# Nine layer norms transposed by VectorE through DRAM, the second MLP matmuls one tile later, and one group's reads spread out

## The chip, the cores and the metric

The kernel runs on one core of a Trainium2 chip. The metric is the device time of one execution in microseconds (us). The time before is the median of three runs. "Span" is the time from the first to the last instruction of the profiled execution.

## What is computed

Two pairs of layers run one after the other on 2048 tokens of width 512: attention with 32 heads of width 16, then a dense layer of 1792 features with the Mish activation. Each of the four starts with a layer norm of its input and adds its result to it.

```python
x = x + A(layernorm(x));  x = x + B(layernorm(x))      # twice, with the same weights
# A: qkv = x @ wqkv; p = softmax(q k^T / 4); o = p v; o @ wo
# B: h = x @ w1 + b1; act = h * tanh(softplus(h)); act @ w2
```

## The kernel before

**Tiling.** The tokens are cut into four chunks `c` of 512, each of four blocks of 128. TensorE (PE) contracts over partitions, so each norm's result is needed with features on the partitions: 4 tiles of 128 features by 512 tokens, each split into a high part `th` and the rest `tl`. A product takes three matmuls (high by high, high by low, low by high), which is `mm3` at L176 to L181.

**A norm** is `norm_parts` (L183). VectorE (DVE) takes the statistics (L211, L212), GpSimd (POOL) the root (L190, L191), DVE scales 128 tokens to `xn` (L201), PE transposes them in four matmuls with an identity into one PSUM bank (L247), ScalarE (ACT) copies the bank to `th` (L173) and DVE subtracts to get `tl` (L174). The names are `tpm`, `thm` for the norms ahead of the MLP and `tpq`, `thq` for those ahead of attention. `spread` hangs a norm's steps on the MLP's tiles. It is used for nine norms: chunks 1 to 3 ahead of each MLP, and chunks 0 to 2 ahead of the second attention, which run within the last chunk of the first MLP.

**Attention's input.** `qkv` goes through 32 (feature tile, chunk) pairs `(m, c)`, each 12 matmuls into one of three PSUM banks of the pool "s". ACT and DVE split the bank into `pt` (L173, L174), and ACT's DMA queue writes it to DRAM as `scr` (L525). As soon as m = 0 and 4 are done for all chunks, `prep_qk(0)` reads the first group of heads back. It has 28 steps of one DMA each. The first 14 (two heads) go out on the queues of SP and POOL, the last 14 on ACT's queue and in program order. `2 * PREP` = 14 steps are taken at once, and then two after each further pair. From m = 6 on, `some_max` takes row maxima of the scores in between (PE L336, DVE L340).

**The MLP** runs 14 feature tiles `f` for each chunk in turn. `hid` is 12 matmuls of w1 (L179 to L181, `h`), followed by a chain of ACT, DVE and POOL instructions that makes `ah` (L659) and `al` (L661). `outp` is 12 matmuls of w2 (L673, `mo`), the first 8 with `ah`, the last 4 with `al`. `LAG` = 2 sets the order: after `hid` of tile i and its hooks comes `outp` of tile i - 2. The buffers `he` and `hr` are single, `hb`, `ah` and `al` double.

**The first tiles of an MLP.** The output projection of the last chunk of attention is not ready when the MLP starts. Its operands come by DMA (`num`, and `rec` through POOL's queue), DVE multiplies them (L604), ACT copies the product to `oh` (L610) and DVE subtracts to get `ol` (L611). Its 48 matmuls with wo are hung in four quarters of 12 on tiles 5 to 8 of chunk 0, right after `hid` and ahead of that step's `outp`. The third matmul of a quarter reads `ol`.

**Order.** All PE instructions stand in program order, which `att.pe` fixes. Those given to `behind` (or a `pin`) keep program order too. The rest is placed by a scheduler from its own model of times, and each engine and DMA queue then works through its list in that fixed order.

Of the kernel before, what the change touches and what calls it, by code (L numbers as in the profile page):

```python
# [9 lines left out]
F32 = mybir.dt.float32  # L10
# [8 lines left out]
P = 128  # L19
# [22 lines left out]
PRE = 4  # L42
FILL = 12
KEEP = 2
PREP = 7
WARM = (4, 1, 1)
GSTEPS = NCH * NKT
STEPS = NG * GSTEPS
HEADS = STEPS * HG
LAG = 2  # L50
MAX_M = (6, 3, 7)
T_BUFS = {"he": 1, "hr": 1}
NBLK = 22
# [15 lines left out]
def kernel(ctx: ExitStack, tc: tile.TileContext, x, wqkv, wo, w1, b1, w2, out):  # L69
# [24 lines left out]
    def b8(shape, dt, name):  # L94
        return blk.tile(shape, dt, tag="blk", name=name)
# [18 lines left out]
    def t512(tag, name, dt=F32):  # L114
        return tmp.tile([P, 512], dt, tag=tag, name=name, bufs=T_BUFS.get(tag, 2))
# [60 lines left out]
    def mm3(acc, pairs, first=True, last=True, pe=lambda ins: ins):  # L176
        n = len(pairs)
        for i, (ah, al, bh, bl) in enumerate(pairs):
            pe(nc.tensor.matmul(acc, ah, bh, start=first and i == 0, stop=False))  # L179
            pe(nc.tensor.matmul(acc, ah, bl, start=False, stop=False))  # L180
            pe(nc.tensor.matmul(acc, al, bh, start=False, stop=last and i == n - 1))  # L181

    def norm_parts(src, nm, got, key, tag, fine=False, pin=lambda ins: ins, pe=lambda ins: ins, halves=False):  # L183
        st = tmp.tile([P, NCH, 6], F32, tag="st", name=f"st{nm}")
        mv = tmp.tile([P, NCH, 2], F32, tag="mv", name=f"mv{nm}")
        ve = tmp.tile([P, NCH], F32, tag="ve", name=f"ve{nm}")
        rs = tmp.tile([P, NCH], F32, tag="rs", name=f"rs{nm}")

        def rstd(t, n):
            nc.gpsimd.tensor_scalar(ve[:, t : t + n], mv[:, t : t + n, 1], EPS, None, op0=ALU.add)  # L190
            nc.gpsimd.tensor_tensor(rs[:, t : t + n], ve[:, t : t + n], mhalf[:, t : t + n], op=ALU.pow)  # L191

        xns = []

        def scaled(t, tag):
            if tag == "raw":
                xn = tmp.tile([P, 2, 512], F32, tag=tag, name=f"xn{nm}{t}", bufs=3)[:, 0]
            else:
                xn = t512(tag, f"xn{nm}{t}")
            pin(  # L200
                nc.vector.tensor_scalar(  # L201
                    xn, src[:, t], mv[:, t, 0:1], rs[:, t : t + 1], op0=ALU.subtract, op1=ALU.mult
                )
            )
            return xn

        def next_scaled():
            xns.append(scaled(len(xns), ("f", "ah")[len(xns) // 2]))

        for t in range(NCH):  # L210
            pin(nc.vector.bn_stats(st[:, t], src[:, t]))  # L211
            pin(nc.vector.bn_aggr(mv[:, t], st[:, t]))  # L212
            if fine:
                rstd(t, 1)
                if t and tag == "mx":
                    next_scaled()
        if not fine:
            rstd(0, NCH)
        yield
        th = b8([P, KT, CW], F32R, f"th{nm}")  # L220
        tl = b8([P, KT, CW], F32R, f"tl{nm}")
        got[key] = (th, tl)
        if tag == "mx":
            while len(xns) < NCH:
                next_scaled()
            yield
            for u in range(NCH // 2):
                tp = ps.tile([P, 2, 512], F32, tag=tag, name=f"tp{nm}{u}")
                for e in range(2):
                    for k in range(KT):  # L230
                        pe(nc.tensor.transpose(tp[:, e, ts(k, P)], xns[2 * u + e][:, ts(k, P)], ident))
                two = ts(u, 2 * P)
                split_psum(
                    th[:, :, two].rearrange("p k (t n) -> p k t n", n=P),
                    tl[:, :, two].rearrange("p k (t n) -> p k t n", n=P),
                    tp.rearrange("p t (k n) -> p k t n", n=P),
                    pin,
                )
                yield
            return  # L240
        for t in range(NCH):
            xn = scaled(t, "raw" if tag == "acc" else "f")
            if halves:
                yield
            tp = pbank(tag, f"tp{nm}{t}")
            for k in range(KT):
                pe(nc.tensor.transpose(tp[:, ts(k, P)], xn[:, ts(k, P)], ident))  # L247
            split_psum(th[:, :, ts(t, P)], tl[:, :, ts(t, P)], tp.rearrange("p (k n) -> p k n", k=KT), pin)
            yield

    def spread(hooks, c, f0, src, nm, got, key, pe):
        parts = norm_parts(src, nm, got, key, "acc", pe=pe, halves=True)
        for i in range(2 * NCH + 1):
            hooks.setdefault((c, f0 + i // 2), []).append(lambda: next(parts, None))

    class Attention:
        def __init__(self, l, scr):
# [18 lines left out]

        def prep_qk(self, g):
            l = self.l
            ks, qs = [], []
            for u in range(HG // 2):  # L280
                k = b8([P, S], F32R, f"ks{l}{g}{u}")
                q = b8([P, S], F32R, f"qs{l}{g}{u}")
                m, h0 = divmod(g * HG + 2 * u, P // DH)
                for e in range(2):
                    r0 = e * HALF
                    queue = nc.sync
                    pin = lambda ins: ins
                    if g == 0 and u:
                        queue, pin = nc.scalar, behind
                    elif g == 0 and e:  # L290
                        queue = nc.gpsimd
                    pin(queue.dma_start(
                        k[r0 + KROWS : r0 + MROWS].bitcast(F32).rearrange("p (r n) -> p r n", n=P),
                        minus[:, None, :].to_broadcast([MROWS - KROWS, S // P, P]),
                    ))
                    yield
                    for t, parts, base in ((k, K_PARTS, NCH), (q, Q_PARTS, 0)):
                        for j, a in enumerate(parts):
                            pin(queue.dma_start(
                                t[r0 + j * DH : r0 + (j + 1) * DH].bitcast(F32),  # L300
                                self.scr[base + m][a, (h0 + e) * DH : (h0 + e + 1) * DH, :].bitcast(F32),
                            ))
                            yield
                ks.append(k)
                qs.append(q)
            self.qk[g] = (ks, qs)

        def prep_v(self, g, cs=range(NCH)):
            if g not in self.va:
# [113 lines left out]
        def drain(self):  # L423
            b, self.full = self.full, None
            if b is None:
                return
            g, qb = divmod(b, NCH)
            ot = t512("f", f"ot{self.l}{b}")
            nc.scalar.activation(ot, self.accs.pop(b), AF.Copy)
            nc.sync.dma_start(self.oscr[qb][g // 2, g % 2], ot)  # L430

        def run(self, hooks, pre, fill):
# [203 lines left out]
    def mlp(l, x2s, w1t, w2t, tts, dst, hooks, pe):  # L636
        acts, obs = {}, {}

        def hid(c, f):
            th, tl = tts[c]  # L640
            w = w1t[f // 2]
            acc = pbank("s", f"h{l}{c}{f}")
            mm3(
                acc,
                [(w[:, 0, k, ts(f % 2, P)], w[:, 1, k, ts(f % 2, P)], th[:, k, :], tl[:, k, :]) for k in range(KT)],
                pe=pe,
            )
            nm = f"{l}{c}{f}"
            hb, e, r = t512("f", "hb" + nm), t512("he", "he" + nm), t512("hr", "hr" + nm)
            nc.scalar.activation(hb, acc, AF.Identity, bias=b1t[:, f : f + 1])  # L650
            nc.vector.tensor_scalar(e, hb, HCLAMP, None, op0=ALU.min)  # L651
            nc.scalar.activation(e, e, AF.Exp)  # L652
            nc.vector.scalar_tensor_tensor(e, e, 2.0, e, op0=ALU.add, op1=ALU.mult)  # L653
            nc.scalar.activation(r, e, AF.Ln, bias=1.0, scale=0.5)  # L654
            nc.scalar.activation(r, r, AF.Exp, bias=lnhalf, scale=-1.0)  # L655
            mul = nc.vector if (l, c) == (1, NCH - 1) and f >= FT - 2 else nc.gpsimd
            mul.tensor_tensor(hb, hb, e, op=ALU.mult)  # L657
            ah, al = t512("ah", "ah" + nm, F32R), t512("al", "al" + nm, F32R)
            nc.vector.tensor_tensor(ah, hb, r, op=ALU.mult)  # L659
            mul.tensor_tensor(hb, hb, r, op=ALU.mult)  # L660
            nc.vector.tensor_tensor(al, hb, ah.bitcast(F32), op=ALU.subtract)  # L661
            acts[c, f] = (ah, al)

        def outp(c, f):
# [81 lines left out]
    for l in range(2):  # L746
# [96 lines left out]
            on(f2, lambda i=i: load_w2(i - 1))  # L843
        on(9, lambda: load_w2(6))
        for c in range(NCH - 1):
            spread(hooks, c, 5 if c else 0, x2s[c + 1], f"m{l}{c + 1}", tts, c + 1, att.pe)
        wts, tt = {}, {}
        if l == 0:
            last = NCH - 1
            for f, js in ((2, (0,)), (4, (2,)), (9, (1,)), (11, (3,)), (12, (4,)), (13, (5,))):  # L850
                hooks.setdefault((last, f), []).append(lambda js=js: load_qkv(1, wts, js, splits))
            for c in range(last):
                spread(hooks, last, 1 + 4 * c, x2s[c], f"q1{c}", tt, c, att.pe)
        mlp(l, x2s, w1t, w2t, tts, xs if l == 0 else out, hooks, att.pe)
    close_banks()

# [27 lines left out]
```

## Time and profile before

| | |
|---|---|
| median of three runs (lowest, highest) | 3557.0 us (3555.14, 3560.2) |
| the profiled execution: time, span | 3557.3 us, 3555.5 us |
| matmul instructions | 28716 |
| VectorE, ScalarE, POOL busy | 83%, 71%, 15% of the span |
| first attention's input | about 8 to 120 us |
| first attention, with its output projection | to about 1449 us |
| first MLP | 1449 to 1789 us |
| second attention's input, second attention | to about 3220 us |
| second MLP | 3220 to 3554 us |

In a timeline row the first number is the start, the second the duration, and the brackets hold how long the engine sat idle before the row and what ended that. Matmuls overlap, so their spacing counts and not their duration: the span divided by 28716 is not the cost of any of them, while two neighbours of 512 columns start 0.23 us apart.

### The profile page before, as it was taken

Reading aid. Unit: us, or ns where it says so; the run is one execution under the profiler, and the core shown is the slowest. Engines: PE = TensorE matmul, PEld = TensorE weight load, DVE = VectorE, ACT = ScalarE, POOL = GpSimd, SP = SyncE. Lnnn points to the kernel's source line nnn. Section 1 sums busy time; section 2 is a strip of 40 time slices with the busy share of each in tenths; the row PEclk is TensorE's granted clock in tenths of the full one; section 3 lists DMA queues with packets and bytes.
Section 4 is the critical chain, followed back from the end, with each engine's and each line's share of the span. In section 5 each row is a group of like instructions: output and inputs, shape, how many; then the busy total and the mean of one; then the engine's idle time right before and its main releaser. Section 6 shows DMA issues by size and latency. Waiting matters only on the chain.

```text
span 3555.5 us, 69179 instructions
## 1 busy us (share of the span) xinstructions
PE 3531.8 (99%) x28716; PEld 1940.7 (55%) x28716; DVE 2941.3 (83%) x3016; ACT 2522.2 (71%) x3401; POOL 532.8 (15%) x612
## 2 busy tenths in 40 slices
PE   9999999999999999999999999999999999999999
PEld 7644444444444444788776444444444444447887
DVE  5789999999999994656646999999999999946544
ACT  3188888888888887344422888888888888873444
POOL 3100000000100002444411000000000000024443
PEclk9999999999999999999999999999999999999999
DMA  7641312213132124500164212112021111246000
GB/s 249 219 97 47 83 44 76 61 51 71 46 78 49 42 80 70 186 32 13 60 214 146 53 31 45 38 29 44 29 38 38 41 35 35 74 74 202 13 13 24
DMA packets 139430, 255.11 MB, mean 72 GB/s; under 512 B 29348, under 2 KB 73316, under 8 KB 125292
## 3 DMA queue, kind: packets, MB, share of 16 engines
q1 hardware_dynamic: 112196, 174.04, 19.5%
q10 hardware_dynamic: 19176, 43.06, 3.4%
q0 software_dynamic: 7744, 33.60, 3.4%
q8 instruction: 225, 3.69, 0.5%
q14 instruction: 89, 0.73, 0.1%
HBM read 149.43 MB, written 100.14 MB: 70 GB/s over the span
## 4 chain that ended last, share of the span: by engine, by line
PE 95%; DVE 2%; DMA 2%; issue 1%; ACT 1%; POOL 1%; ACTq 0%; DVEq 0%; SPq 0%; POOLq 0%
PE pv L410 30%; PE pm L336 17%; PE ss L394 12%; PE sp L384 9%; PE mo L673 8%; PE h L179 3%; PE h L181 3%; PE h L180 3%; PE qk L179 1%; PE qk L180 1%; PE qk L181 1%; PE va L179 1%; PE wo L179 1%; DMA scr<-pt 1%; PE va L181 1%
## 5 line engine op out<-in xcount | busy, mean ns | idle before, releaser
L340 DVE TENSOR_REDUCE mxv<-pm 128x2 f32<-128x1024 f32 x2048 | 2385.8, 1219 | 137.3 <-PE pm L336 86.9
L385 ACT ACTIVATE p<-sp 128x1024 f32<-128x1024 f32 x1366 | 1395.9, 1022 | 19.6 <-PE sp L384 15.7
L410 PE MATMUL pv<-p,va 128*32 128x256 f32 (+2 forms) x16032 | 1166.9, 392 | 0.1
L336 PE MATMUL pm<-ks,qs 48*128 48x512 f32 x4096 | 1095.5, 446 | 0.4
L395 ACT ACTIVATE p<-ss 128x512 f32<-128x512 f32 x1364 | 815.1, 598 | 347.4 <-PE ss L394 254.9
L384 PE MATMUL sp<-qs,ks 50*128 50x512 f32 x2732 | 724.8, 446 | 0.7 <-ACT p L385 0.4
L336 PEld LDWEIGHTS pm<-ks,qs 48*128 48x128 f32 x4096 | 451.1, 184 | 345.7 <-issue 171.3
L410 PEld LDWEIGHTS pv<-p,va 128*32 128x32 f32 x16032 | 367.7, 108 | 494.7 <-issue 416.9
L394 PE MATMUL ss<-qs,ks 50*128 50x512 f32 x1364 | 611.4, 448 | 0.0
L394 PEld LDWEIGHTS ss<-qs,ks 50*128 50x128 f32 x1364 | 252.0, 185 | 329.5 <-ACT p L395 225.5
L384 PEld LDWEIGHTS sp<-qs,ks 50*128 50x128 f32 x2732 | 261.2, 183 | 202.4 <-ACT p L385 120.3
L355 POOL CAST np<-nt 128x32 fp32r<-128x32 f32 x64 | 13.4, 210 | 2213.2 <-DVE nt L353 2213.2
L659 DVE TENSOR_TENSOR ah<-hb,hr 128x512 fp32r<-128x512 f32 x112 | 77.3, 690 | 137.2 <-ACT hr L655 89.0
L650 ACT ACTIVATE hb<-h,b1t 128x512 f32<-128x512 f32 x112 | 77.1, 688 | 142.4 <-PE h L181 140.3
L657 POOL TENSOR_TENSOR hb<-hb,he 128x512 f32<-128x512 f32 x110 | 145.7, 1325 | 205.1 <-DVE he L653 202.6
L660 POOL TENSOR_TENSOR hb<-hb,hr 128x512 f32<-128x512 f32 x110 | 147.3, 1339 | 123.7 <-DVE ah L659 123.7
L654 ACT ACTIVATE hr<-he 128x512 f32<-128x512 f32 x112 | 70.8, 632 | 109.8 <-DVE he L653 94.7
L173 ACT ACTIVATE pt<-qk 128x512 fp32r<-128x512 f32 x64 | 38.0, 597 | 154.0 <-PE qk L181 110.9
L652 ACT ACTIVATE he<-he 128x512 f32<-128x512 f32 x112 | 70.8, 632 | 93.5 <-DVE he L651 89.1
L651 DVE TENSOR_SCALAR he<-hb 128x512 f32<-128x512 f32 x112 | 69.3, 619 | 79.9 <-ACT hb L650 77.5
L661 DVE TENSOR_TENSOR al<-hb,ah 128x512 fp32r<-128x512 f32 x112 | 83.0, 741 | 24.7 <-POOL hb L660 24.5
L174 DVE TENSOR_TENSOR pt<-qk,pt 128x512 fp32r<-128x512 f32 x64 | 43.6, 685 | 61.8 <-ACT pt L173 61.8
(222 smaller groups left out, 3110.9 us busy)
## 6 DMA issues: line engine op xcount, KB each, us to landing
scr<-pt ACTq DMA_DIRECT2D x64, 512.0 KB
qs<-scr SPq DMA_DIRECT2D x174, 128.0 KB
ks<-scr SPq DMA_DIRECT2D x174, 128.0 KB
vscr<-v SPq DMA_DIRECT2D x32, 512.0 KB
va<-vscr SPq DMA_DIRECT2D x64, 256.0 KB
oscr<-ot SPq DMA_DIRECT2D x64, 256.0 KB
ww<-sw POOLq DMA_DIRECT2D x14, 1024.0 KB, 4.8
num<-oscr SPq DMA_DIRECT2D x64, 128.0 KB
```

What stands on the lines that cost most here:

```text
L179: pe(nc.tensor.matmul(acc, ah, bh, start=first and i == 0, stop=False))
L181: pe(nc.tensor.matmul(acc, al, bh, start=False, stop=last and i == n - 1))
L336: nc.tensor.matmul(pm[:, e], qs[u][rows, q0 : q0 + P], ks[u][rows, ts(n, 512)], start=True, stop=True)
L340: nc.vector.tensor_reduce(self.mxs[b][:, 2 * u : 2 * u + 2, qt, n], pm, axis=AX.X, op=ALU.max)
L384: self.pe(nc.tensor.matmul(sp[:, e], k, q, start=True, stop=True))
L385: nc.scalar.activation(self.pts[-1][:, 0:n], sp[:, 0:n], AF.Exp, scale=SCALE)
L394: self.pe(nc.tensor.matmul(sp, k, q, start=True, stop=True))
L395: nc.scalar.activation(self.pts[i // 3][:, 2], sp, AF.Exp, scale=SCALE)
L410: nc.tensor.matmul(self.accs[b][ts(h, VW), cols], self.va[b // NCH][:, kt, h, :], self.pts[j][:, e, cols], start=kt == 0 and q0 == 0, stop ...
L657: mul.tensor_tensor(hb, hb, e, op=ALU.mult)
L660: mul.tensor_tensor(hb, hb, r, op=ALU.mult)
L673: nc.tensor.matmul(obs[c][t // 2][:, t % 2], act[:, ts(t, P)], w[:, part, f % 2], start=f == part == 0 and act is ah, stop=f == FT - 1 and ...
```

## The change

Nine norms get a new function, `norm_blocks`. DVE scales 128 tokens of two blocks, transposes them in 32x32 blocks (L283), and four DMAs on SP's queue write the result to a DRAM tensor `turned` in runs of 64 tokens (256 bytes); this is done twice for a chunk. One DMA reads the chunk back with features on the partitions, into the buffer of `tl`. ACT copies it to `th` (L294), and DVE subtracts in place (L295), 512 elements at a time. The tokens come out in another order within the chunk, and three places follow it: `ot` in the second attention, and `ah` and `al` in the MLP for c > 0, which are written in runs of 32 elements.

```diff
-PREP = 7
+PREP = 2
-LAG = 2
+LAG = 3
...
+    def norm_blocks(src, nm, got, key):
+        rs, mv = statistics(src, nm)
+        yield
+        th = b8([P, KT, CW], F32R, f"th{nm}")
+        tl = b8([P, KT, CW], F32R, f"tl{nm}")
+        got[key] = (th, tl)
+        raw = tl.bitcast(F32)
+        turned = dram.tile([D, CW], F32, name=f"nt{nm}")
+        for h in range(2):
+            xn = tmp.tile([P, 2, D], F32, tag="raw", name=f"xn{nm}{h}", bufs=3)
+            for j in range(2):
+                t = h + 2 * j
+                nc.vector.tensor_scalar(
+                    xn[:, j], src[:, t], mv[:, t, 0:1], rs[:, t : t + 1], op0=ALU.subtract, op1=ALU.mult
+                )
+            y = tmp.tile([P, D // TR, 2, TR], F32, tag="raw", name=f"y{nm}{h}", bufs=3)
+            for j in range(2):
+                nc.vector.transpose(y[:, :, j], xn[:, j].rearrange("p (b r) -> p b r", r=TR))
+            for a in range(P // TR):
+                n0 = h * CW // 2 + a * 2 * TR
+                nc.sync.dma_start(
+                    turned[:, n0 : n0 + 2 * TR].rearrange("(b q) n -> q b n", q=TR),
+                    y[ts(a, TR)].rearrange("q b j r -> q b (j r)"),
+                )
+            yield
+        nc.sync.dma_start(raw, turned.rearrange("(k p) n -> p k n", p=P))
+        yield
+        for k in range(KT):
+            nc.scalar.activation(th[:, k], raw[:, k], AF.Copy)
+            nc.vector.tensor_tensor(tl[:, k], raw[:, k], th[:, k].bitcast(F32), op=ALU.subtract)
+            if k % 2:
+                yield
+
-    def spread(hooks, c, f0, src, nm, got, key, pe):
-        parts = norm_parts(src, nm, got, key, "acc", pe=pe, halves=True)
-        for i in range(2 * NCH + 1):
-            hooks.setdefault((c, f0 + i // 2), []).append(lambda: next(parts, None))
+    def spread(hooks, c, f0, src, nm, got, key):
+        parts = norm_blocks(src, nm, got, key)
+        for i in range(6):
+            hooks.setdefault((c, f0 + i), []).append(lambda: next(parts, None))
...
+            if self.l and qb < NCH - 1:
+                nc.scalar.activation(mixed(ot), grouped(acc), AF.Copy)
...
+            if c:
+                nc.vector.tensor_tensor(mixed(ah), grouped(hb), grouped(r), op=ALU.mult)
+                mul.tensor_tensor(hb, hb, r, op=ALU.mult)
+                nc.vector.tensor_tensor(mixed(al), grouped(hb), mixed(ah.bitcast(F32)), op=ALU.subtract)
...
-                spread(hooks, last, 1 + 4 * c, x2s[c], f"q1{c}", tt, c, att.pe)
+                spread(hooks, last, (1, 5, 8)[c], x2s[c], f"q1{c}", tt, c)
```

`LAG` = 3 puts `outp` of tile i - 3 behind `hid` of tile i. `PREP` = 2 takes 4 steps of `prep_qk(0)` at once, and two after each further pair as before. `prep_qk` now enters its buffers in `self.qk` at the start, so that maxima can be emitted while its steps are still under way. Nothing else is changed: the norms of chunk 0 ahead of each MLP, and those ahead of the first attention and of chunk 3 ahead of the second, stay with PE, and the quarters of the output projection stay on tiles 5 to 8.

More of the change, by code (lines that the diff above doesn't have):

```diff
@@ L181, in mm3, with statistics @@
             pe(nc.tensor.matmul(acc, al, bh, start=False, stop=last and i == n - 1))
+    def statistics(src, nm):
+        st = tmp.tile([P, NCH, 6], F32, tag="st", name=f"st{nm}")
+        mv = tmp.tile([P, NCH, 2], F32, tag="mv", name=f"mv{nm}")
+        ve = tmp.tile([P, NCH], F32, tag="ve", name=f"ve{nm}")
+        rs = tmp.tile([P, NCH], F32, tag="rs", name=f"rs{nm}")
+        for t in range(NCH):
+            nc.vector.bn_stats(st[:, t], src[:, t])
+            nc.vector.bn_aggr(mv[:, t], st[:, t])
+        nc.gpsimd.tensor_scalar(ve, mv[:, :, 1], EPS, None, op0=ALU.add)
+        nc.gpsimd.tensor_tensor(rs, ve, mhalf, op=ALU.pow)
+        return rs, mv
     def norm_parts(src, nm, got, key, tag, fine=False, pin=lambda ins: ins, pe=lambda ins: ins, halves=False):
@@ L195, in scaled @@
         def scaled(t, tag):
[L196 to L199, printed above, removed]
+            xn = t512(tag, f"xn{nm}{t}")
             pin(
@@ L241, in norm_parts @@
         for t in range(NCH):
-            xn = scaled(t, "raw" if tag == "acc" else "f")
+            xn = scaled(t, "f")
             if halves:
@@ L249, in norm_parts, with mixed, grouped @@
             yield
-    def spread(hooks, c, f0, src, nm, got, key, pe):
-        parts = norm_parts(src, nm, got, key, "acc", pe=pe, halves=True)
-        for i in range(2 * NCH + 1):
-            hooks.setdefault((c, f0 + i // 2), []).append(lambda: next(parts, None))
+    def mixed(t):
+        return t.rearrange("p (j g r) -> p g j r", j=2, r=TR)
+    def grouped(t):
+        return t.rearrange("p (g j r) -> p g j r", j=2, r=TR)
+    def norm_blocks(src, nm, got, key):
[34 more added lines that the diff above has]
+            hooks.setdefault((c, f0 + i), []).append(lambda: next(parts, None))
     class Attention:
@@ L278, in prep_qk @@
             l = self.l
-            ks, qs = [], []
+            ks, qs = self.qk[g] = [], []
             for u in range(HG // 2):
@@ L282, in prep_qk @@
                 q = b8([P, S], F32R, f"qs{l}{g}{u}")
+                ks.append(k)
+                qs.append(q)
                 m, h0 = divmod(g * HG + 2 * u, P // DH)
@@ L303, in prep_qk @@
                             yield
-                ks.append(k)
-                qs.append(q)
-            self.qk[g] = (ks, qs)
         def prep_v(self, g, cs=range(NCH)):
@@ L428, in drain @@
             ot = t512("f", f"ot{self.l}{b}")
-            nc.scalar.activation(ot, self.accs.pop(b), AF.Copy)
+            acc = self.accs.pop(b)
+            if self.l and qb < NCH - 1:
+                nc.scalar.activation(mixed(ot), grouped(acc), AF.Copy)
+            else:
+                nc.scalar.activation(ot, acc, AF.Copy)
             nc.sync.dma_start(self.oscr[qb][g // 2, g % 2], ot)
@@ L658, in hid @@
             ah, al = t512("ah", "ah" + nm, F32R), t512("al", "al" + nm, F32R)
-            nc.vector.tensor_tensor(ah, hb, r, op=ALU.mult)
-            mul.tensor_tensor(hb, hb, r, op=ALU.mult)
-            nc.vector.tensor_tensor(al, hb, ah.bitcast(F32), op=ALU.subtract)
+            if c:
+                nc.vector.tensor_tensor(mixed(ah), grouped(hb), grouped(r), op=ALU.mult)
+                mul.tensor_tensor(hb, hb, r, op=ALU.mult)
+                nc.vector.tensor_tensor(mixed(al), grouped(hb), mixed(ah.bitcast(F32)), op=ALU.subtract)
+            else:
+                nc.vector.tensor_tensor(ah, hb, r, op=ALU.mult)
+                mul.tensor_tensor(hb, hb, r, op=ALU.mult)
+                nc.vector.tensor_tensor(al, hb, ah.bitcast(F32), op=ALU.subtract)
             acts[c, f] = (ah, al)
@@ L845 @@
         for c in range(NCH - 1):
-            spread(hooks, c, 5 if c else 0, x2s[c + 1], f"m{l}{c + 1}", tts, c + 1, att.pe)
+            spread(hooks, c, 5 if c else 0, x2s[c + 1], f"m{l}{c + 1}", tts, c + 1)
         wts, tt = {}, {}
```

## The prediction

> **What bounds the kernel now.** I read the page's first part, then PE's waits, then the chain of waits in order of time, then timelines at each hole. The page says that PE is the bound:
>
> ```profile
> PE 3531.8 (99%) x28716; PEld 1940.7 (55%) x28716; DVE 2941.3 (83%) x3016; ACT 2522.2 (71%) x3401; POOL 532.8 (15%) x612
> ```
>
> So an instruction taken from PE is time saved as long as nothing else comes late, and there are only 23.7 us in which PE is idle. The waits of PE (total, times, longest) name the ones after the start:
>
> ```profile
> PE qk L179 <- DVE pt L174: 4.3, 2, 2.4
> PE tpq L247 <- DVE tlq L174: 3.4, 1, 3.4
> PE mo L673 <- DVE al L661: 2.3, 3, 1.2
> ...
> PE mo L673 <- DVE ah L659: 1.3, 1, 1.3
> ```
>
> **1. Transposes leave PE.** In the chain of waits the starts of one tile's w2 matmuls and the next give the length of a tile. The first two rows have no norm between them, the last two hold one group of four transposes:
>
> ```profile
> 1510.59 2.80 PE mo L673 x12
> ...
> 1516.14 2.80 PE mo L673 x12
> ...
> 1566.12 2.80 PE mo L673 x12
> 1572.11 2.80 PE mo L673 x12
> ```
>
> A plain tile takes 5.55 us, one with a group 5.99, so a group costs 0.44. Nine norms have 4 groups each: 36 x 0.44 = **-15.8 us**. The wait of 3.4 us for `tlq` ended a transpose and goes with it: **-3.4**.
>
> **2. w2 three tiles behind.** In the first tiles of each MLP PE waits for `ah` and `al`. With one `hid` more (2.73 us) ahead of each `outp` the longest of these waits, 1.3, is covered: 2.3 + 1.3 = **-3.6**. The work itself stays the same. The last tile has no wait before, so the end gains nothing.
>
> **3. Reads spread out.** The two waits for `pt` are one in each layer's attention input. ACT's timeline shows why:
>
> ```profile
> 74.45 0.60 ACT L173 ACTIVATE pt<-qk 128x512 fp32r<-128x512 f32 x1 [8.51 <-DMA scr<-pt]
> ```
>
> ACT stood 8.51 us behind reads that it issues itself and that wait for `scr` to land; three banks filled and PE stopped:
>
> ```profile
> 73.02 0.39 PE L181 MATMUL qk<-thq,sqkv 128*128 128x512 f32 x1
> 75.83 0.80 PE L179 MATMUL qk<-thq,sqkv 128*128 128x512 f32 x1 [2.42 <-DVE pt L174]
> 76.42 0.63 PE L180 MATMUL qk<-tlq,sqkv 128*128 128x512 f32 x1
> ```
>
> The hole costs more than itself. Behind it matmuls start 0.43 us apart instead of 0.23 for some 3 us (granted clock 0.50 from 76 to 78). From 70 to 80 us PE starts 28 matmuls instead of 46: 18 x 0.23 = 4.1, of which 1.7 is the clock. The second layer has 29 from 1840 to 1850: 3.9, of which 2.0 is the clock. Together 8.0. In the built order the first read on ACT's queue now stands four pairs (11 us) later, when `scr` has landed, and two or three reads stand between two copies. They still wait for free DMA slots, so I take 7 of the 8 (bounds 0 and 8): **-7.0**.
>
> **4. What comes late next.** This step gives time back. The quarters stay on tiles 5 to 8, but PE gets there earlier. Before, it had by then done 6 `hid`, 3 `outp`, 4 groups and 1.2 us of waits. These are DVE's rows and PE's first quarter:
>
> ```profile
> 1469.56 0.68 DVE L661 TENSOR_TENSOR al<-hb,ah 128x512 fp32r<-128x512 f32 x1
> 1470.44 2.29 DVE L604 TENSOR_TENSOR num<-num,rec 128x2048 f32<-128x2048 f32 x1 [0.20 <-issue]
> ...
> 1474.72 2.38 DVE L611 TENSOR_TENSOR ol<-num,oh 128x2048 fp32r<-128x2048 f32 x1 [0.33 <-ACT oh L610]
> ```
>
> ```profile
> 1476.83 0.39 PE L179 MATMUL wo<-wo0l,oh 128*128 128x512 f32 x1
> 1477.05 0.39 PE L180 MATMUL wo<-wo0l,oh 128*128 128x512 f32 x1
> 1477.28 0.40 PE L181 MATMUL wo<-wo0l,ol 128*128 128x512 f32 x1
> ```
>
> `ol` ends at 1477.1 and is read at 1477.28: nothing to spare. After the change PE starts the MLP at the same 1448.7 and comes to that matmul after 6 x 2.73 + 2 x 2.8 + 0.5 = 22.5 us, at 1471.2. In the built order `num` still stands behind `al` of tile 2 on DVE, so `ol` can't come earlier by the change. DVE has more to do ahead of it: 8 transposes and one `xn` more, four `tl` less. For a transpose of 512 columns the trace has only the narrow one:
>
> ```profile
> L353 DVE STREAM_TRANSPOSE nt<-folded 128x32 f32<-128x32 f32 x64 | 13.1, 205 | 2.7 <-DVE folded L349 0.5
> ```
>
> The bounds are 0.45 us (the scaling of 512, which L201 shows uncontended) and 16 x 0.205 = 3.3. I take 0.7, near the 0.60 to 0.69 of DVE's other passes over 512. This gives 8 x 0.7 + 0.5 - 4 x 0.6 = +3.7 us on DVE, which sits idle for 5.7 us of this stretch. I let half of it through: `ol` at 1478.9, PE waits 7.7 us, and the clock costs another 1.8 as in step 3. Two layers: 2 x 9.5 = **+19.0**. It is a wait in place of those of step 2.
>
> **5. What is hidden.** Transposes elsewhere lie beside DVE's idle time (4 to 7 tenths busy in the MLP slices). Steps on ACT and DVE for `th` and `tl` are as many as before. `ah`, `al` and `ot` in runs of 32: `tlm` from runs of 128 takes 682 ns against 685 for a plain pass, so I take 0 (bounds 0 and double, another 0.7 twice a tile, in a chain with 5.55). The 81 new DMAs take SP 0.33 us each. Moved past on SP's queue: the w14 load, at 1448.88 before, now stands behind the writes of chunk 2's norm (about 1478), and is needed at tile 8, near 1500. The new wait is that of L294 and L295 for the load; behind them stand ACT's `hr` and DVE's `al` of tile 5, which PE needs three quarters later. For the writes the nearest rows are the 16-partition loads of `rec` at 135 to 148 GB/s (1408 to 1413 us) and full ones at 410: a half, 512 KB, takes 1.3 to 3.9 us, the load of 1 MB 2.6, and a tile or more lies between them. I take 0.
>
> By the Trainium skill ("DMA: Bandwidth & Descriptors", Specifications) transfers below 512 B are read, modified and written, which speaks against runs of 256 B; by its rule alone the writes would be slower than 3.9 us, and the second rival below holds what that would cost. No row of this trace shows 256 B writes by themselves.
>
> **Sum.** -15.8 - 3.4 - 3.6 - 7.0 + 19.0 = -10.8. The profiled execution took 3557.3 (1.8 around its span of 3555.5), close to the median 3557.0: **3546.5 us**, 0.3% faster. With `ol` at 1477.1 it is 3543; with all 3.7 us late and 2.5 more from collisions with POOL, 3555. Such collisions show already: an `al` beside POOL's `hb` takes 1.77 instead of 0.68.
>
> ```profile
> 1465.15 1.77 DVE L661 TENSOR_TENSOR al<-hb,ah 128x512 fp32r<-128x512 f32 x1 [1.19 <-POOL hb L660]
> ```
>
> By the Trainium skill ("SBUF — State Buffer", Who interferes with whom) a DVE instruction with two SBUF inputs and a GpSimd one that reads SBUF exclude each other. The row agrees, and the new `tl`, which reads SBUF twice where it read PSUM once, would fall under it.
>
> **Rivals.**
> - *The quarter does not wait* (0.16): `ol` is ready by 1471, as DVE is rid of its waits for transposes. Then the 19.0 go: 3527.5; with a wait of 2 us each 3532. Against it: `num` stands behind the third tile's `al`, and the sum of DVE's rows grew.
> - *The trip through DRAM comes late* (0.14), slower than before: L294 and L295 hold ACT and DVE in order, and nothing of tile i can pass. It decides when a load lands later than one tile and the extra tile of slack, 11 us after its issue. At 5 us beyond for six norms without quarters beside them it costs 30: 3576. For it: the first load stands behind 2 MB of weights. Against it: step 5's 3.9 and 2.6.
> - *Transposes at 3.3 us* (0.05): 8 x 2.6 more ahead of `ol` in each layer, 3546.5 + 42 = 3588.
> - *The reads only move their hole* (0.13): four pairs later ACT stands as long, and step 3 gives 0 or 1: 3553.
>
> My forecast has 0.52. **Range** 3530 to 3562: it holds the forecast's bounds, most of the first rival and the last. A measurement can tell about 0.2%, 7.1 us, from no change. The forecast is faster in 0.40 and within 0.2% in 0.12, the first rival is faster, the last within: faster 0.57, same 0.25, slower 0.18.
>
> **What would show it.** PE rows: no L247 `tpq` in the MLP, tiles of 5.55 throughout, no wait for `pt` of 2 us, and in both MLPs one wait of `wo` L181 for `ol` of 6 to 10 us with slow matmuls behind it. A transpose near 0.7 us; loads that land before L294 gets to them. The prediction is wrong if `ol` is early, if `mo` waits for `ah` or `al` in chunks 1 to 3, or if L294 waits for its load while PE stands.

## The result, and the profile after

The changed kernel takes 3566.9 us (median of 9 runs, 3565.5 to 3567.7) against 3555.2 for the kernel before (9 runs of the same session, 3553.1 to 3560.2): ratio 1.0030, interval 1.0020 to 1.0041. The forecast was 3546.5, with a range up to 3562. It is 0.3% slower where 0.3% faster was forecast. The profiled execution has a span of 3565.7 us, 10.1 more than before.

The first part of the page after (busy time, share, instructions):

```profile
PE 3524.6 (99%) x28572; PEld 1931.1 (54%) x28572; DVE 3028.7 (85%) x3052; ACT 2519.1 (71%) x3401; POOL 571.0 (16%) x612
```

PE has 144 matmuls and 7.2 us of busy time less, and the span is longer all the same: PE stands more. VectorE is busy for 87 us more. Most of that is not new work: its 112 `al` take 152.5 us instead of 83.0, because most of them now run beside an instruction of POOL. PE's waits after (total, times, longest) say where:

```profile
PE wo L179 <- ACT oh L661: 13.0, 2, 6.5
PE mo L729 <- DVE x L739: 9.7, 6, 4.3
PE wo L181 <- DVE ol L662: 2.3, 2, 1.2
...
PE mo L729 <- DVE al L717: 1.6, 4, 0.8
PE mo L729 <- DVE al L713: 1.6, 1, 1.6
```

The waits for `pt` and `tlq` are gone. The wait of the wo quarter is there, 15.3 us with both rows. The wait of w2 for `x` is new, and no step of the prediction has it. Line 739 is the addition that takes a chunk's finished sums out of their PSUM banks (L683 before); the next chunk's first w2 matmul needs those banks.

**The reads.** Where PE started 28 matmuls from 70 to 80 us, it now starts 47, at full clock (columns: width, PE busy and matmuls, granted clock, DMA share, GB/s):

```profile
70.00:80.00 10.00, 10.00 (x47) 1.00 0.81 285
```

In ACT's timeline the copies to `pt` stand 2.9 us behind a read instead of 8.51, less than three banks hold:

```profile
74.06 0.60 ACT L173 ACTIVATE pt<-qk 128x512 fp32r<-128x512 f32 x1 [2.92 <-DMA ks<-minus]
```

**The tiles.** Starts of w2 in the chain of waits: 5.55 us apart, now also through the tiles that had transposes.

```profile
1506.71 2.79 PE mo L729 x12
1512.27 2.79 PE mo L729 x12
1517.82 2.79 PE mo L729 x12
```

**The head of the MLP.** VectorE's rows ahead of the first quarter, and then PE's:

```profile
1468.45 0.68 DVE L717 TENSOR_TENSOR al<-hb,ah 128x512 fp32r<-128x512 f32 x1
1469.05 3.35 DVE L655 TENSOR_TENSOR num<-num,rec 128x2048 f32<-128x2048 f32 x1
1472.32 1.29 DVE L283 STREAM_TRANSPOSE ym<-xnm 128x512 f32<-128x512 f32 x2
1473.55 0.38 DVE L702 TENSOR_SCALAR he<-hb 128x512 f32<-128x512 f32 x1
1473.85 0.67 DVE L715 TENSOR_TENSOR ah<-hb,hr 128x512 fp32r<-128x512 f32 x1
1474.45 2.28 DVE L662 TENSOR_TENSOR ol<-num,oh 128x2048 fp32r<-128x2048 f32 x1
```

```profile
1474.40 0.80 PE L179 MATMUL wo<-wo0l,oh 128*128 128x512 f32 x1 [6.49 <-ACT oh L661]
1476.78 0.79 PE L181 MATMUL wo<-wo0l,ol 128*128 128x512 f32 x1 [1.16 <-DVE ol L662]
```

`num` takes 3.35 us where it took 2.29 (POOL works on `hb` beside it), and it starts 24.4 us after the start of the MLP (1444.67) instead of 21.8. `ol` ends 32.0 us after that start instead of 28.4, in the second MLP 32.5 instead of 29.3. The two transposes between `num` and `ol` cost at most 0.1, since ACT's `oh`, which `ol` reads, ends only at 1474.3. PE arrives 23.2 us after the start. The clock behind the two waits:

```profile
1474.00:1484.00 10.00, 8.44 (x22) 0.58 0.93 329
```

**The start of a chunk.** The longest wait for `x`, on PE and on VectorE:

```profile
1640.35 3.78 PE L729 MATMUL mo<-w20l,ah 128*128 128x512 f32 x8 [4.26 <-DVE x L739]
```

```profile
1634.62 1.77 DVE L713 TENSOR_TENSOR al<-hb,ah 128x512 fp32r<-128x512 f32 x1 [1.18 <-POOL hb L712]
...
1637.28 0.43 DVE L702 TENSOR_SCALAR he<-hb 128x512 f32<-128x512 f32 x1 [0.89 <-ACT hb L701]
1637.62 0.68 DVE L711 TENSOR_TENSOR ah<-hb,hr 128x512 fp32r<-128x512 f32 x1
...
1638.40 0.69 DVE L704 SCALAR_TENSOR_TENSOR he<-he 128x512 f32<-128x512 f32 x1
...
1639.01 2.48 DVE L739 TENSOR_TENSOR x<-mo,x 128x512 f32<-128x512 f32 x4
```

The sums that L739 reads were complete when the next `hid` began, at 1633.2. It starts 5.8 us later because four of the MLP's own instructions stand ahead of it on VectorE's list, and those wait for one another.

**Account by stages**, from the starts of the `hid` tiles (after less before): start of the first MLP -4.0; from there to tile 8 +5.7 and +5.3 in the two MLPs; the rest of the first MLP -2.7, of the second +3.0; from the first MLP's tile 12 of chunk 3 to the second MLP 0.0; the end +2.7. Together +10.1, but for rounding. With three tiles of lag, one `outp` (2.8 us) moves out of each head; it comes back at the end and, in the first MLP, ahead of the second attention.

### The profile page after: what moved, and what is told of

Read it like the earlier page. It is cut to its first block, busy times and chain, and to the rows that moved or that the text cites. A ratio compares the mean times of both kernels' runs of the same rounds, so it can differ in the third digit from the quotient of the medians.

```text
span 3565.7 us, 69085 instructions
## 1 busy us (share of the span) xinstructions
PE 3524.6 (99%) x28572; PEld 1931.1 (54%) x28572; DVE 3028.7 (85%) x3052; ACT 2519.1 (71%) x3401; POOL 571.0 (16%) x612
## 4 chain that ended last, share of the span: by engine, by line
PE 89%; DVE 5%; POOL 2%; ACT 2%; issue 1%; DMA 1%; DVEq 0%; ACTq 0%; POOLq 0%
PE pv L457 30%; PE pm L383 17%; PE ss L441 13%; PE sp L431 9%; PE mo L729 6%; PE qk L179 2%; PE h L179 2%; PE h L181 2%; PE h L180 2%; PE qk L180 1%; PE qk L181 1%; POOL hb L712 1%; DVE al L713 1%; PE wo L179 1%; PE va L179 1%
## 5 line engine op out<-in xcount | busy, mean ns | idle before, releaser
L713 DVE TENSOR_TENSOR al<-hb,ah 128x512 fp32r<-128x512 f32 x84 | 122.6, 1459 | 72.4 <-POOL hb L712 70.0
L712 POOL TENSOR_TENSOR hb<-hb,hr 128x512 f32<-128x512 f32 x82 | 139.1, 1696 | 204.0 <-ACT he L703 139.7
L702 DVE TENSOR_SCALAR he<-hb 128x512 f32<-128x512 f32 x112 | 52.6, 470 | 84.7 <-ACT hb L701 62.7
L701 ACT ACTIVATE hb<-h,b1t 128x512 f32<-128x512 f32 x112 | 76.9, 687 | 64.4 <-DVE al L713 28.4
L704 DVE SCALAR_TENSOR_TENSOR he<-he 128x512 f32<-128x512 f32 x112 | 82.0, 732 | 21.4 <-ACT he L703 14.0
```

What stands on the lines that cost most here:

```text
L713: nc.vector.tensor_tensor(mixed(al), grouped(hb), mixed(ah.bitcast(F32)), op=ALU.subtract)
```

## The experiments

Theory A: the wait for `x` comes with `LAG` = 3. Theory B: it comes from the norms' work on VectorE. Theory C, formed after the first eight: the early transposes are VectorE's new backlog. All ratios are to the kernel before on the same chip, in brackets the 95% interval; its median was 3555.8 to 3558.8 in these sessions.

### Parts of the change alone

**e1**, the kernel before with three tiles:

```diff
-LAG = 2
+LAG = 3
```

> The kernel before with the second matmuls three tiles behind; norms and reads as before. Theory A (the accumulators' addition L683 is late because w2 stands one tile further back while ah and al keep two buffers, so that VectorE's chain is tied to the end of the same outp as the addition): matmuls of w2 wait for x at each chunk's end, 1 us or more in each of six places, about 10 us with slow matmuls behind them. The quarter comes 2.8 us earlier and waits 2.5 us for ol in each layer, 8 us with the clock. The waits for ah and al go, -3.6. Together 3569 us. Theory B (the addition is late because VectorE has the transposes to do): no wait for x, 3560 us.

Measured: 3576.5 us, 1.0057 (1.0044 to 1.0071). Waits for `x` only 2.0 us, for `oh` and `ol` 11.8, and a new one of 6.1 for the statistics of a norm (`mvq`) in chunk 3. Slower than either theory said, and not where A said: three tiles alone make little of the wait for `x`, but they cost 20 us in all.

**e2**, the kernel before with the reads spread out (`PREP` = 2, and the buffers entered in `self.qk` at the start).

> The kernel before with only the reads of the first group spread out. The two waits for pt of 2.4 and 1.9 us go and the spacing of matmuls behind them is even: 46 matmuls from 70 to 80 us instead of 28, together -8.0 us, 3547 us. Rival (the hole only moves): PE waits for pt later, 3555 us.

Measured: 3549.9 us, 0.9981 (0.9972 to 0.9989). In the trace the first MLP starts 3.3 us earlier and the second 6.9. 46 matmuls start from 70 to 80 us. The holes are gone and did not move; the gain is 6.4 us, of 8.0 expected here and 7.0 in the prediction.

**e3**, the changed kernel with `LAG` = 2 and `PREP` = 7, so that the norms and the order in which `prep_qk` enters its buffers differ from before; **e4**, the changed kernel with `LAG` = 2.

> The changed kernel with w2 two tiles behind and the reads in one go, so that only the nine norms differ from before. Transposes -15.8, the wait for tlq with its clock -5.0. The quarter still comes 5 us too early for ol, whose work on VectorE begins later: 2 x (5 + 2.7) = +15.4. Theory A: no wait for x, 3550 us. Theory B: the waits for x stay, 9.7 us and 16.4 with the clock, 3566 us.

> The changed kernel with w2 two tiles behind. Against it with three: waits for oh and ol shorter by 2.8 us in each layer, waits for al at the head of the MLP back to 2 to 3.6 us. Theory A: the waits of w2 for x (9.7 us) go, 3542 us. Theory B: they stay, 3558 us.

Measured: e3 3560.5 us, 1.0011 (1.0003 to 1.0020); e4 3554.7, 0.9994 (0.9986 to 1.0003). In both the wait for `x` shrinks from 9.7 to 2.5, but w2 waits for `ah` (2.3) and `al` (3 to 5) in its place, and `oh` and `ol` still cost 7.5. Another 3.6 to 3.7 us of waits of w2, in the first tiles of the MLPs, are put down to no engine. Both times lie between the theories: neither part alone makes the loss. The nine norms win nothing in e3.

### Moving the quarters, a third buffer

**e5**, the changed kernel with `for f in range(7, 11)` for the quarters, and **e8**, the same with `LAG` = 2.

> The changed kernel with the four quarters of the output projection on tiles 7 to 10 instead of 5 to 8. PE then comes to the first of them some 33 us after the start of the MLP, and ol ends 32 us after it: the waits for oh and ol (15.3 us) and the slow matmuls behind them (7.8) go, 3567 - 23 = 3544 us. Rival (ol depends on where PE stands and moves with the quarter, or the additions and the last chunk's norm come late): half or less of it, 3555 us or more.

> The changed kernel with w2 two tiles behind and the quarters on tiles 7 to 10. Theory A: no wait for x, none for oh and ol, the waits for al at the head of the MLP back: 3567 - 16 - 23 + 3 = 3531 us. Theory B: 3547 us.

Measured: e5 3560.5 us, 1.0012 (1.0004 to 1.0021); e8 3564.9, 1.0025 (1.0015 to 1.0035). In e5 the waits for `oh` and `ol` are gone, and of their 23 us 6 are won: w2 now waits 14.9 for `x` instead of 9.7, 8.7 for `al` and `ah` at the head instead of 1.6. In e8 a load of w2 weights comes late as well (6.9); why was not followed up. In e5 the wait had moved on, so PE's meeting with `ol` was not the only limit: VectorE was still behind at the next tiles and at the chunks' starts.

**e6**, the changed kernel with three buffers of `ah` and `al` and `NBLK` = 21, and **e7**, the same with the quarters on tiles 7 to 10.

> The changed kernel with three buffers of ah and al instead of two, paid for with one of 22 large blocks. Theory A (two buffers tie VectorE's chain to the end of the last outp of the chunk): the waits of w2 for x (9.7 us, 16.4 with the clock) go, 3550 us. Theory B (VectorE is late because of the transposes and reordered writes): they stay, 3567 us. The waits for oh and ol stay in both.

> Both: three buffers of ah and al, quarters on tiles 7 to 10. Theory A: 3567 - 23 - 16 = 3528 us. Theory B: 3544 us.

In the traces of these two half the clock was granted for a part (e6) or nearly all (e7) of the first attention, and the medians are 3660 and 3696 us, so only the waits in the MLPs are read, where tiles take 5.55 us as elsewhere. The wait for `x` is 2.7 and 3.6 us instead of 9.7 and 14.9. That fits A, but VectorE's list changed with the buffers too, and in a way that matters (see "The order alone"). The shortest run of e6, with a granted clock of 0.996, took 3559.8 us, between the two theories.

### Where the norms stand on VectorE

**e9** (`LAG` = 2) and **e10** (`LAG` = 3) put no transpose ahead of `num` and `ol`:

```diff
-                nc.vector.tensor_scalar(
+                behind(nc.vector.tensor_scalar(
...
-                nc.vector.transpose(y[:, :, j], xn[:, j].rearrange("p (b r) -> p b r", r=TR))
+                behind(nc.vector.transpose(y[:, :, j], xn[:, j].rearrange("p (b r) -> p b r", r=TR)))
...
-            spread(hooks, c, 5 if c else 0, x2s[c + 1], f"m{l}{c + 1}", tts, c + 1)
+            spread(hooks, c, 5, x2s[c + 1], f"m{l}{c + 1}", tts, c + 1)
```

> The changed kernel with w2 two tiles behind, and with the scalings and transposes of the nine norms kept in program order on VectorE, the first norm begun at tile 5 instead of 0, so that no transpose stands ahead of num and ol. Theory C (the head of the MLP and the starts of the chunks are limited by VectorE's backlog, of which the transposes placed early are the part that is new): ol ends 28 to 29 us after the start of the MLP instead of 33, the waits for oh and ol (7.5 us, 11 with the clock) shrink to 1 or 2, and the waits at the starts of chunks 2 and 3 (10 us) halve: 3554.7 - 10 - 5 = 3540 us. Rival (the backlog is that of the MLP's own chain, and a transpose only fills its idle time): 3550 us or more.

> The same with w2 three tiles behind. PE comes 2.8 us earlier to the quarter than with two, which the wait for oh takes back: 5 us in each layer, 7 with the clock. Theory A (three tiles with two buffers of ah cost 6.4 us at the chunks' starts, as in the kernel before): 3540 + 2 x 5 + 6 - 3 = 3553 us. Rival (once VectorE is rid of the early transposes, three tiles are no worse): 3545 us or less.

Measured: e9 3545.8 us, 0.9966 (0.9954 to 0.9979); e10 3582.4, 1.0069 (1.0057 to 1.0082). In e9 no wait for `x` is left, more than C expected, and the time is nearer to C than to its rival. But C is not confirmed: `ol` ends 30.0 and 31.5 us after the MLPs' starts and not 28 to 29, `oh` and `ol` still cost 5.1 and not 1 to 2, and 5.8 us of its gain are missing. The expectation for e10 failed by 29 us. `LAG` alone parts the two kernels by 36.6 us, and e10 waits for `x` at all six chunk starts:

```profile
PE mo L729 <- DVE x L739: 21.1, 6, 5.1
```

What separates them is seen in e10's timeline of VectorE, POOL and ACT at one of the six:

```profile
1716.68 1.78 POOL L712 TENSOR_TENSOR hb<-hb,hr 128x512 f32<-128x512 f32 x1 [2.64 <-ACT he L703]
...
1718.49 1.77 DVE L713 TENSOR_TENSOR al<-hb,ah 128x512 fp32r<-128x512 f32 x1 [1.19 <-POOL hb L712]
...
1720.35 0.69 ACT L701 ACTIVATE hb<-h,b1t 128x512 f32<-128x512 f32 x1 [0.47 <-DVE al L713]
1721.14 0.43 DVE L702 TENSOR_SCALAR he<-hb 128x512 f32<-128x512 f32 x1 [0.89 <-ACT hb L701]
1721.49 0.68 DVE L711 TENSOR_TENSOR ah<-hb,hr 128x512 fp32r<-128x512 f32 x1
...
1722.34 1.74 POOL L712 TENSOR_TENSOR hb<-hb,hr 128x512 f32<-128x512 f32 x1 [2.63 <-ACT he L703]
1722.87 2.48 DVE L739 TENSOR_TENSOR x<-mo,x 128x512 f32<-128x512 f32 x4
```

Each row waits for the one above: POOL's `hb`, `al`, the next-but-one tile's `hb` in the buffer that `al` frees, its `he`, then `ah` of the tile between, which needs nothing of that but stands behind `he` in VectorE's list, and POOL again. From POOL to POOL it is 5.66 us, and PE needs 5.55. A loop longer than PE's tile never makes up what is put into it, and each chunk puts the addition, the statistics and a norm into it. In the lists of the kernel before and of e9, which have `LAG` = 2, `ah` stands ahead of that `he` in nearly every tile, and in all of the last five ahead of the addition at each of the six chunk starts: the loop does not exist there. The changed kernel's list is in e10's order in the last two tiles ahead of each of them.

**e11**, e9 with the norms ahead of the second attention begun earlier (`(1, 2, last)[c], (8, 8, 6)[c]`), and **e12**, e10 with the quarters on tiles 6 to 9.

> The first of these with the three norms ahead of the second attention begun at tile 8 of chunk 1, tile 8 of chunk 2 and tile 6 of chunk 3 instead of tiles 1, 5 and 8 of chunk 3, so that no chunk has more than two norms. If VectorE's load in chunk 3 is what is left, the waits for al there (about 1.5 us) go, and it is 1 to 3 us below the first; if the buffers that are held longer cost something, above it.

> Three tiles behind, norms in program order from tile 5 on, and the quarters on tiles 6 to 9. PE comes to the first quarter 28 us after the start of the MLP, when ol has just ended: the waits for oh and ol are under 1.5 us. If the stall is only a matter of that meeting, 3553 - 12 = 3541 us. If it is VectorE's backlog, the wait moves to ah and al of the next tiles as it did with the quarters on tiles 7 to 10, and it is 3547 us or more.

Measured: e11 3554.8 us, 0.9994 (0.9985 to 1.0003), 9 us above e9: w2 waits 12.3 for `al` and `ah` all through chunks 1 to 3. Early is no better; the middle chunks have a norm already, but that this is the reason is not shown. e12 3566.1, 1.0026 (1.0015 to 1.0036): 16 us below e10. The quarter waits 3.2 instead of 13.0 and nothing new appears at the tiles behind it, while the waits for `x` stay (19.5), as the loop would have it.

### The order alone

**e13** is e10, **e17** the changed kernel itself, each with one rule and nothing else: `he` of a tile stands behind `ah` of the tile before, on VectorE's list.

```diff
...
-            nc.vector.tensor_scalar(e, hb, HCLAMP, None, op0=ALU.min)
+            low = nc.vector.tensor_scalar(e, hb, HCLAMP, None, op0=ALU.min)
+            if before:
+                tc.add_manual_dep(
+                    low.ins,
+                    before[0].ins.name,
+                    mybir.DependencyInfo(mybir.DependencyClass.NoSync, mybir.DependencyReason.DATA),
+                    reason="issue order",
+                )
...
-                nc.vector.tensor_tensor(mixed(ah), grouped(hb), grouped(r), op=ALU.mult)
+                before[:] = [nc.vector.tensor_tensor(mixed(ah), grouped(hb), grouped(r), op=ALU.mult)]
...
```

> Three tiles, norms pinned from tile 5 on as in the run of 3582 us, and one rule more for VectorE's list: he of a tile stands behind ah of the tile before. If the serial chain al, hb, he, ah, POOL's hb (5.67 us a tile) is the cause, the waits for x shrink from 21.1 us to under 5 and the time to 3582 - 30 = 3552 us. If three tiles with two buffers are the cause whatever the order, the waits for x stay above 12 us and the time above 3570.

> The changed kernel with the one rule for VectorE's order and nothing else. If the order is the cause of its waits for x (9.7 us, 16.7 with the clock), they shrink to under 3 us and the time to 3567 - 14 = 3553 us. If they come from the norms' work placed early, they stay at 6 us or more and the time above 3560.

Measured: e13 3548.2 us, 0.9976 (0.9965 to 0.9986); e17 3547.9, 0.9970 (0.9960 to 0.9981). The waits for `x` are gone in both, with two buffers and three tiles unchanged. The waits of PE in e17:

```profile
PE wo L179 <- ACT oh L661: 13.1, 2, 6.9
PE wo L181 <- DVE ol L662: 4.5, 2, 2.2
PE vp L179 <- DVE mxv L387: 1.7, 2, 0.9
```

The order is the cause: 34 us in e10, 19 in the changed kernel (21 by the ratios of the two sessions). The rule is the only edit, but the scheduler lays every list anew: with `he` and `ah` left out, about 30 of VectorE's 2828 other instructions stand elsewhere too. With the loop gone `al` takes 0.68 us again in e17, and VectorE is busy for 2964.7 us instead of 3028.7.

Counted in the traces, the later tile's `he` stands ahead of the earlier tile's `ah` at this many of the 110 steps from one tile to the next in the two MLPs:

| runs | steps |
|---|---|
| `LAG` = 3, two buffers: changed kernel, e1, e5, e10, e12 | 92, 94, 90, 96, 94 |
| `LAG` = 3, three buffers: e6, e7 | 18, 20 |
| `LAG` = 2: before, e2, e3, e4, e8, e9, e11, e14, e15, e16 | 6 to 18 |
| the rule: e13, e17, e18 | 0 |

So the order comes with three tiles and two buffers together, also without the new norms (e1). A reading that fits: w2 of tile i - 2 then stands behind `hid` of tile i + 1 and reads the buffer that `ah` of tile i needs, so `he` of tile i + 1 can run before `ah` of tile i may start. In e17, where `ah` must go first, VectorE waits for PE's w2 ahead of `ah` in 44 places, 93.7 us in all, and PE's tiles in chunks 1 to 3 take 5.55 us all the same. Theory A falls in the form in which it was stated (three tiles with two buffers cost time whatever the order): what they bring is the order. B falls too: the norms' work is what the loop could not absorb, not what made it.

### A better version

**e14**, **e15** and **e16** start from e9: quarters on tiles 6 to 9, the last three norms on tiles 1, 4 and 7, and both. **e18** is e13 with the quarters on tiles 7 to 10.

> The run of 3545.8 us (two tiles, norms pinned) with the quarters on tiles 6 to 9. If PE only meets ol too early there, the waits for ol (4.7 us, 7 with the clock) go: 3539 us. If VectorE's backlog is the limit, they come back as waits for ah or al or for a weight load behind it: 3545 us or more.

> The run of 3545.8 us with the norms ahead of the second attention begun at tiles 1, 4 and 7 of chunk 3 instead of 1, 5 and 8. If its waits for al near the end of chunk 3 (4.3 us) come from the last norm's subtractions, which come late, they go: 3541 us. If it is VectorE's load in the whole chunk, they only move: 3546 us.

> Both of these, the quarters on tiles 6 to 9 and the last three norms begun at tiles 1, 4 and 7: 3535 us if each works by itself.

> Three tiles, norms pinned from tile 5 on, the rule for VectorE's order, and the quarters on tiles 7 to 10. Against the run of 3548 us with the quarters on 5 to 8: its waits for oh and ol (13.8 us, 20 with the clock) go: 3528 us. If they come back as waits for ah, al or a weight load, 3538 us or more.

Measured: e14 3538.4 us, 0.9946 (0.9933 to 0.9958); e15 3544.5, 0.9963 (0.9950 to 0.9975); e16 3537.7, 0.9944 (0.9932 to 0.9957); e18 3529.0, **0.9920** (0.9906 to 0.9933), below both kernels. Here a moved quarter does win its wait (7.4 us in e14, 19 in e18), as it had not in e5 and e8. The rule for the order is not the reason: e12 won 16 us with the loop in its list. What e12, e14 and e18 share, and e5 and e8 lack, is that no transpose of the new norms stands in the first five tiles of an MLP; the changed kernel with the rule and moved quarters was not run. e15's waits for `al` near the end of chunk 3 only moved. PE's longest waits in e18:

```profile
PE qk L179 <- DVE pt L174: 1.7, 1, 1.7
PE vp L179 <- DVE mxv L387: 1.7, 2, 0.9
PE warm L798 <- DVE warm L793: 1.4, 1, 1.4
PE tpm L256 <- DVE xnm L210: 0.7, 2, 0.4
```

## Why the prediction was wrong, point by point

- **Transposes leave PE, -15.8: right.** The pairs of tiles that took 11.96 to 12.02 us take 11.11. The wait for `tlq`, forecast -3.4, was worth 5.0 with the slow matmuls behind it (the pair of tiles took 17.00 among neighbours of 11.97).
- **w2 three tiles behind, -3.6: half right, and the step that failed.** The waits for `ah` and `al` at the heads fell from 3.6 to 1.6. But "the work itself stays the same" looked at PE alone. The same constant rearranged VectorE's list, and the rows at the chunks' starts lost 16.6 us over PE's pure 11.11 per pair (7 rows in the two MLPs, 94.4 against 77.8), for which the sum had no term. e17 gives 19 us back by the order alone, and its ratio of 0.9970 is the 0.3% that was forecast, in part because other errors cancel. Step 5 shares the fault: it counted VectorE's idle time (4 to 7 tenths busy) as room. In a list that is worked through in order, idle time that lies inside a loop of 5.66 us is no room.
- **Reads, -7.0: right**, by e2 (-6.4) and by the stage starts. The step's reason for 7 instead of 8, that reads wait for free DMA slots, is not told apart from other waits by any row; ACT's copy stood 2.9 us behind a read.
- **The wait of the quarter, +19.0: right in kind, 4 short.** The waits are 15.3 for the two layers against 15.4 forecast, by luck, as two errors cancel: `ol` ended 32.0 us after the MLP's start instead of 30.2, and PE arrived after 23.2 instead of 22.0. `ol` was late because `num` started 2.6 us later, which is the step's own cause, and took 1.1 longer beside POOL, which the step had only in its upper bound. PE waited first and longest for `oh` (6.5), and not for `ol`. The clock cost 3.9 and 4.0 by pairs of tiles, instead of 1.8 each.
- **A transpose at 0.7: right** (median 0.698). The rival with 3.3 falls.
- **The trip through DRAM, taken as 0: right for PE.** L294 waited 8.2 us in two places for its load, and no PE row waits for `th` or `tl` of these norms. In the first, the load went out at 1475.6 and ACT came past it at 1485.2, near the 11 us from which the second rival decides. The Trainium skill's rule on transfers below 512 B ("DMA: Bandwidth & Descriptors", Specifications) would speak for that rival; no run here separates its share from that of the weights in the same queue.
- **The rivals.** None of the four is what happened. The one that ended slower had the wrong mechanism: it looked for the loss in DRAM and it lay in VectorE's list. Of the signs that were named for a wrong prediction one showed: `mo` waited once for `al` in chunk 3 of the first MLP, 1.6 us, which is not where the time went. The chances add up to 0.56, 0.25 and 0.19, not to 0.57, 0.25 and 0.18.
- **The sum of the misses.** 16.6 at the chunks' starts, 4.3 of clock behind the quarters and 1.6 of waits that stayed at the heads, less 1.6 more won with `tlq`, make 20.9 us. That is what lies between the forecast's -10.8 and the spans' +10.1.

What stays open: whether the scheduler laid the order for the reason given above, since its model of times isn't in the trace; and what made e1 lose 20 us. Its list is in the loop's order, and new waits for `oh`, `ol`, `mvq` were seen, but e1 was not run with the rule.

## What to carry to other kernels

A constant that shifts one engine's program order can let a scheduler rearrange the list of another, as it did here; compare those lists before and after, and look in them for an instruction that stands behind another it doesn't need. Add up the loop that buffers and list order close (here `al`, `hb`, `he`, `ah`, POOL: 5.66 us) and hold it against the bound engine's period (5.55): a loop that is longer can hide nothing that is added to it. An engine's busy time is not its work: of VectorE's 87 us more, 70 were `al` that took longer beside POOL, and that went with the loop. When a wait is taken away and the time hardly moves (23 us of waits and clock, 6 us won in e5), look for what else makes the engine behind it late, here the loop (e17) and the norms in the first tiles (e12), and mend that first.

## What the runs showed of the hardware

- What a wait costs PE beyond itself grows with its length. From the tile pairs of the changed kernel: waits of 0.82, 1.15 and 1.19 us lengthened a pair by 1.34, 1.67 and 1.71, each 0.5 more, with a granted clock of 1.00 around them. 2.05 and 4.26 us cost 4.08 and 6.90, 2.0 and 2.6 more, with 0.57 and 0.50 granted behind them. Two waits that end 2.4 us apart (6.49 and 1.16, with one of 0.17 in the same pair) cost 3.9 more. The stretches at half clock that go with these waits last 3.41, 6.83 and 10.24 us, which is one, two and three times 3.41. The Trainium skill ("TensorE: Matmul & The Clock Gate", What's actually happening) lets the clock fall after an idle window of about 3.4 us; here 2.05 us were enough.
- A DVE instruction over 2048 elements beside POOL took 3.35 us instead of 2.29, as `al` takes 1.77 instead of 0.68. In e10's loop `al` is met by POOL's next `hb`, and that is 1.1 of the 5.66 us.
